# The zero-padded k stationaries of the tails: copied by DVE instead of POOL

## The chip, the cores and the metric

The kernel runs on one core of one Trainium2 chip. The metric is the device time of one execution in microseconds. The engines are TensorE (PE in the profile; its weight loads are PEld), VectorE (DVE), ScalarE (ACT), GpSimd (POOL) and SyncE (SP), which issues the DMAs. Each engine works through its own queue in order, and an instruction that waits for a semaphore holds up those behind it on its engine.

## The reference

An attention with capped scores feeds a gated block. Shapes: q, k, v are 4 x 12 x 448 x 64; x is 4 x 448 x 768; w_in is 768 x 1024, w_sg 448 x 448, w_out 512 x 768, all in float32.

```python
scores = scale * np.matmul(q, k.transpose(0, 1, 3, 2))
scores = cap * np.tanh(scores / cap)
scores = scores - np.max(scores, axis=-1, keepdims=True)
attn = np.exp(scores)
attn = attn / (np.sum(attn, axis=-1, keepdims=True) + 1e-09)
x = np.matmul(attn, v)                    # heads side by side: 448 x 768
h = gelu(x @ w_in)                        # tanh form
u, v = h[..., :512], h[..., 512:]
v_n = (v - mean(v)) / sqrt(var(v) + 1e-06) * g_ln
v_s = np.einsum('ts,bsd->btd', w_sg, v_n) + b_sg[None, :, None]
out = x + (u * v_s) @ w_out
```

## The kernel before

The attention works on pairs of heads: 4 batches of 6 pairs, 24 pairs P in all. A sequence of 448 is three full chunks of 128 keys and a tail of 64 (TL). Each pair has four steps, one for each chunk and one for the tail, in which the tails of both heads share one step of 128 rows. For the pairs after the first the order of a pair's steps is chunk 1, tail, chunk 2, chunk 3 (`unit`, L219). `scores` (L223) writes the scores of one step into one of two PSUM tiles sc; `soft` (L252) and `soft2` (L258) do tanh and exp on ACT into a slot raw; `av` (L266) multiplies with v into pav; `den` (L283) sums the rows on PE, after DVE has added some of the chunks together (`add`, L325, the L328 of the trace).

The scores are made more exact than one pass would be: q and k are split into a rounded part and a rest. Four steps of preparation for the next pair run inside each pair: `prep_a` (q rounded, qs), `prep_k` (k rounded, kh, L172), `prep_b` (rest of q, L180), `prep_c` (rest of k, kl, L188). For the batches 0 and 1 the roundings are on DVE, later on ACT (L157 and L159 in `cast`); the rests are on DVE. For the full chunks PE takes its weights straight from kh and kl (L243). For the tail it takes them from kt (L229): a single buffer of 128 x 2 x 3 x 64, whose middle block is zero, with the tail of head 0 in the first block and that of head 1 in the third. A window of two blocks is then one head's 64 columns beside 64 zero columns, so that the four matmuls of a tail (kh and kl for each head) add up in one tile with the two heads in different rows. The zeros are set once (L694). Two copies fill the blocks for each pair: `kt_hi` (L190) from kh and `kt_lo` (L191) from kl, each 128 x 2 x 64. Each must wait until the tail matmuls of the pair before have read kt.

The gated block of a batch is woven into the attention of the batches after it. `filler` (L551) takes a number of matmuls from a generator between the steps: `norm` (division by den, L365 and L368, and the split of x, L372 to L375), `hv` (L399; gelu and the normalisation, L382 to L426), `hu` (L443; gelu, with L388 writing u), `vsg` (L457, then L466 to L473), `outp` (L486, L491). The weights win, wout and wsg arrive as 64-bit words read by DMA and are decoded while the attention runs (`decode`, L583): one piece is L591 or L594 (DVE early, ACT later), L596, L598, L601 and L604 on DVE, L606 on POOL, L611 on DVE, the rounding L157 or L159, and L613 on POOL. So POOL's queue holds the decoding (L606, L613, and L577 for wsg), the inverse roots of the normalisation (L413) and, before the change, the copies into kt.

The order of instructions on each engine is not that of the code: a scheduler of the framework orders the queues when the program is built, from its own estimate of when each operation can run. Moving two instructions to another engine can therefore move others.

Of the kernel before, what the change touches and what calls it, by code (L numbers as in the profile page):

```python
# [53 lines left out]
def kernel(  # L54
# [15 lines left out]
    nc = tc.nc  # L70
    B, NP, _, _, S = q2.shape
    NC = w_sgT.shape[1]
    FC = S // 128
# [37 lines left out]
    kt_hi, kt_lo = [kt[:, i, ::2, :] for i in range(2)]  # L111

    def f32(ap):
        return ap.bitcast(FP32)
# [18 lines left out]
    def two(t):  # L133
        return t.rearrange("p (a s) -> p a s", a=2)

    raws, qks, vs = {}, {}, {}
# [45 lines left out]
    def prep_c(P):  # L182
        if P >= NPAIR:
            return
        kr = two(raws[P][1])
        kl = qk_p.tile([128, 2, S], FP32R, tag="kl", name="kl")
        eng = nc.gpsimd if P // NP in POOL_KL else nc.vector
        eng.tensor_tensor(out=kl, in0=kr, in1=f32(qks[P][1]), op=ALU.subtract)  # L188
        qks[P].append(kl)
        nc.gpsimd.tensor_copy(out=kt_hi, in_=f32(qks[P][1])[:, :, 128 * FC:])  # L190
        nc.gpsimd.tensor_copy(out=kt_lo, in_=f32(kl)[:, :, 128 * FC:])  # L191
        for t in raws.pop(P):
            raw_s.put(t)

# [506 lines left out]
    for g in range(NSTEP + LAG + 2):  # L701
        P, c = divmod(g, NC)
# [13 lines left out]
        if g < NSTEP:  # L716
            soft2(g)
            if c == 0:
                prep_a(P + 1)
                prep_k(P + 1)  # L720
            elif c == 1:
                prep_b(P + 1)
            elif c == 2:
                prep_c(P + 1)
                load_pair(P + 2)
# [95 lines left out]
```

## Time and profile before

| what | value |
|---|---|
| time, median of 3 runs | 468.64 us (468.02 to 470.51) |
| the profiled execution: its time, its span | 467.07 us, 465.1 us |
| busy: PE, PEld | 442.3 us (95%), 291.8 us (63%) |
| busy: DVE, ACT, POOL | 353.0 us (76%), 291.6 us (63%), 99.1 us (21%) |
| granted TensorE clock, mean | 0.992 |

The rows further down are of four kinds. A row of the windows gives the busy time of each engine in one stretch, with the number of instructions, the granted clock of TensorE, the share of DMA and its rate. A row of the groups gives line, engine and operation, what is written from what, the shapes and the count, then the busy time, the mean of one in ns, and the idle time of the engine just before with what ended it. A row of the timeline gives the start in us from the span's start, the length, the engine, line and operation, the count where equal ones follow each other, and in brackets how long the engine had been idle before it and who ended that. On DVE and ACT one instruction's row can begin before the row above ends, so the distance between two starts can be shorter than a length.

### The profile page before, as it was taken

To read this page: it belongs to the slowest core of one execution; us is meant where nothing else is said; L and a number is where in the kernel's file an instruction comes from. 1 tells how busy PE (TensorE), PEld (TensorE's weight loads), DVE (VectorE), ACT (ScalarE), POOL (GpSimd) and SP (SyncE) were. 2 spreads that over 40 slices of the span, in tenths; PEclk is the share of its full clock that TensorE was granted. 3 is DMA by queue.
4 is the path that set the end of the run, shared out by engine and by line. 5 is a ranking of instruction groups with operands and counts; after the bars stand their busy time and mean duration, and the time that the engine had idled before them with its cause. 6 is when DMAs were issued, how large, how long until landed. Compare 5 with 4: busy or idle time off the path is not lost.

```text
span 465.1 us, 5865 instructions
## 1 busy us (share of the span) xinstructions
PE 442.3 (95%) x2024; PEld 291.8 (63%) x2024; DVE 353.0 (76%) x640; ACT 291.6 (63%) x432; POOL 99.1 (21%) x144
## 2 busy tenths in 40 slices
PE   3999989969999989999999999999999999999996
PEld 0435433345475666665677677766676767778986
DVE  4847998999899888698888557788777455678662
ACT  2659868855786759787678676567778661144410
POOL 1415654265443420410030001000010000000000
PEclk9999998999999999999999999999999999999999
DMA  8457745306212442731230321330320001200002
GB/s 236 172 184 227 246 137 170 109 23 183 93 47 103 136 141 86 238 113 62 81 103 0 117 88 55 135 135 0 108 97 8 17 0 39 75 6 1 0 29 91
DMA packets 20749, 45.23 MB, mean 97 GB/s; under 512 B 3056, under 2 KB 6768, under 8 KB 20720
## 3 DMA queue, kind: packets, MB, share of 16 engines
q1 hardware_dynamic: 20720, 44.86, 29.6%
q8 instruction: 16, 0.26, 0.2%
q14 instruction: 13, 0.11, 0.1%
HBM read 39.35 MB, written 5.51 MB: 96 GB/s over the span
## 4 chain that ended last, share of the span: by engine, by line
PE 57%; DVE 5%; POOL 2%; ACT 1%; issue 1%; POOLq 0%; ACTq 0%
PE gp L486 11%; PE gp L443 10%; PE pav L272 9%; PE gp L399 8%; PE gp L457 8%; PE sc L243 6%; PE sc L229 2%; PE den L291 2%; DVE raw L328 1%; POOL wout L613 1%; POOL raw L606 1%; DVE raw L611 1%; PE gp L365 1%; DVE t L351 1%; DVE xu L368 0%
## 5 line engine op out<-in xcount | busy, mean ns | idle before, releaser
L256 ACT ACTIVATE raw<-sc,qsc 128x896 f32<-128x896 f32 (+1 forms) x96 | 86.1, 909 | 49.2 <-PE sc L243 32.6
L272 PE MATMUL pav<-raw,v 128*64 128x448 f32 x384 | 93.4, 561 | 0.0
L259 ACT ACTIVATE raw<-raw,cap_sb 128x896 f32<-128x896 f32 (+1 forms) x96 | 89.7, 944 | 0.9
L399 PE MATMUL gp<-win,r 128*128 128x512 f32 x264 | 66.5, 400 | 3.3 <-DVE r L373 3.0
L443 PE MATMUL gp<-r,win 128*128 128x448 f32 x288 | 64.1, 371 | 1.4 <-DVE u L388 1.0
L486 PE MATMUL gp<-r,wout 128*128 128x448 f32 x288 | 63.7, 371 | 0.9 <-POOL wout L613 0.5
L399 PEld LDWEIGHTS gp<-win,r 128*128 128x128 f32 x264 | 48.6, 189 | 22.5 <-issue 4.9
L443 PEld LDWEIGHTS gp<-r,win 128*128 128x128 f32 x288 | 53.1, 188 | 14.7 <-issue 7.8
L486 PEld LDWEIGHTS gp<-r,wout 128*128 128x128 f32 x288 | 53.0, 188 | 12.1 <-issue 4.3
L243 PE MATMUL sc<-qs,kh 128*128 128x448 f32 x144 | 55.6, 387 | 1.9 <-DVE kh L200 1.8
L272 PEld LDWEIGHTS pav<-raw,v 128*64 128x64 f32 x384 | 24.6, 138 | 50.4 <-issue 37.9
L243 PE MATMUL sc<-qs,kl 128*128 128x448 f32 x144 | 53.6, 374 | 0.0
L328 DVE TENSOR_TENSOR raw<-raw,raw 128x896 f32<-128x896 f32 (+1 forms) x54 | 47.9, 888 | 4.8 <-PE pav L272 3.3
L457 PE MATMUL gp<-wsg,r 128*128 128x448 f32 x176 | 39.8, 371 | 2.6 <-DVE u L388 2.6
L243 PEld LDWEIGHTS sc<-qs,kh 128*128 128x128 f32 x144 | 27.4, 191 | 19.4 <-ACT raw L256 6.9
L457 PEld LDWEIGHTS gp<-wsg,r 128*128 128x128 f32 x176 | 32.4, 188 | 11.1 <-issue 4.2
L291 PE MATMUL den<-raw,ones_sb 128*32 128x448 f32 x216 | 36.9, 573 | 0.3 <-DVE raw L328 0.3
L190 POOL CAST kt<-kh 128x128 fp32r<-128x128 f32 x23 | 11.7, 508 | 117.1 <-PE sc L229 112.2
L413 POOL TENSOR_TENSOR rs<-rs,pw 128x1 f32<-128x1 f32 (+1 forms) x16 | 9.9, 617 | 102.5 <-DVE rs L412 102.5
L243 PEld LDWEIGHTS sc<-qs,kl 128*128 128x128 f32 x144 | 27.6, 191 | 5.8 <-DVE qs L157 2.1
L188 DVE TENSOR_TENSOR kl<-raw,kh 128x896 fp32r<-128x896 f32 x23 | 27.0, 1174 | 3.2 <-PE den L291 1.8
L613 POOL TENSOR_TENSOR win<-xu,win 128x256 fp32r<-128x256 f32 x22 | 22.8, 1039 | 29.3 <-ACT win L159 16.8
(90 smaller groups left out, 564.4 us busy)
## 6 DMA issues: line engine op xcount, KB each, us to landing
raw<-in_q_dram SPq DMA_DIRECT2D x23, 448.0 KB, 3.5
raw<-in_k_dram SPq DMA_DIRECT2D x23, 448.0 KB, 4.5
v<-in_vp_dram SPq DMA_DIRECT2D x24, 256.0 KB, 3.4
xu<-in_w_in_dram SPq DMA_DIRECT2D x22, 256.0 KB, 4.3
out_dram<-xu SPq DMA_DIRECT2D x24, 224.0 KB, 1.9
raw<-in_w_out_dram SPq DMA_DIRECT2D x11, 256.0 KB, 3.5
u<-in_w_sgT_dram SPq DMA_DIRECT2D x4, 224.0 KB, 5.9
raw<-in_w_in_dram SPq DMA_DIRECT2D x2, 256.0 KB, 4.1
```

Source lines behind the costliest of these rows:

```text
L188: eng.tensor_tensor(out=kl, in0=kr, in1=f32(qks[P][1]), op=ALU.subtract)
L243: nc.tensor.matmul(out=sc[:, h, :S], lhsT=w[:, h, 128 * c - 128:128 * c], rhs=qs[:, h, :], start=(i == 0), stop=(i == 1))
L256: nc.scalar.activation(out=prob(g), in_=src, func=ACTF.Tanh, scale=qsc)
L259: nc.scalar.activation(out=prob(g), in_=prob(g), func=ACTF.Exp, scale=cap_sb)
L272: nc.tensor.matmul(out=pav_t[P][64 * h:64 * h + 64, :S], lhsT=w, rhs=two(p_t[g])[:, h if c else 0, :], start=(g % NC == 0), stop=(c == NC ...
L291: nc.tensor.matmul(out=t[32 * j:32 * j + 32, :S], lhsT=ones_sb[:, 0 if c else 1 + h, NP - 1 - P % NP:NP + 31 - P % NP], rhs=two(src)[:, h ...
L328: eng.tensor_tensor(out=a, in0=a, in1=w, op=ALU.add)
L399: yield 1, lambda i=i, c=c, a=a, w=w: nc.tensor.matmul(out=ps, lhsT=a[c][:, t * 128:t * 128 + 128], rhs=win[w][:, c, HF:], start=(i == 0), ...
L443: yield 1, lambda a=a, w=w, c=c, st=st, sp=sp: nc.tensor.matmul(out=ps, lhsT=win[w][:, c, f * 128:(f + 1) * 128], rhs=a[c][:, :S], start=s ...
L457: yield 1, lambda i=i, c=c, a=a, w=w: nc.tensor.matmul(out=ps, lhsT=a[c][:, f * 128:(f + 1) * 128], rhs=wsg[w][:, c, :], start=(i == 0), s ...
L486: yield 1, lambda ps=ps, c=c, a=a, w=w, f=f, st=st, sp=sp: nc.tensor.matmul(out=ps, lhsT=wout[w][:, f, c * 128:(c + 1) * 128], rhs=a[f][:, ...
L613: nc.gpsimd.tensor_tensor(out=dst[1], in0=f, in1=f32(dst[0]), op=ALU.subtract)
```

## The change

In `prep_c` the two copies into kt are issued on DVE (`nc.vector`) instead of POOL (`nc.gpsimd`). Their shapes, sources and destinations stay.

```diff
@@ -187,8 +187,8 @@
         eng = nc.gpsimd if P // NP in POOL_KL else nc.vector
         eng.tensor_tensor(out=kl, in0=kr, in1=f32(qks[P][1]), op=ALU.subtract)
         qks[P].append(kl)
-        nc.gpsimd.tensor_copy(out=kt_hi, in_=f32(qks[P][1])[:, :, 128 * FC:])
-        nc.gpsimd.tensor_copy(out=kt_lo, in_=f32(kl)[:, :, 128 * FC:])
+        nc.vector.tensor_copy(out=kt_hi, in_=f32(qks[P][1])[:, :, 128 * FC:])
+        nc.vector.tensor_copy(out=kt_lo, in_=f32(kl)[:, :, 128 * FC:])
         for t in raws.pop(P):
             raw_s.put(t)
```

The scheduler's order moves on PE, DVE, ACT, POOL and SP. Three places follow; two smaller ones are told in words. On PE the four matmuls of a tail stand together at some places where they were spread, or a little later, and around 229 us of the trace before DVE's L383 and L426 of the normalisation change places. On DVE the two copies of a pair follow kl, mostly with one to four other instructions in between; for the late pairs they stand after instructions that ran when the tail before had ended.

The first place is DVE at about 155 to 165 us of the trace before, where the first batch's u are made (u_99 is the fourth, t_101 its temporary; raw_67, raw_72 and raw_73 are slots with pieces of wout). Before:

```order
L383 SCALAR_TENSOR_TENSOR t_101<-t_101,gp 128x448
L611 TENSOR_TENSOR raw_72<-raw_72 128x256
L596 TENSOR_SCALAR raw_73<-raw_73 128x256
L598 TENSOR_SCALAR raw_73<-raw_73 128x256
L601 SCALAR_TENSOR_TENSOR raw_73<-raw_73 128x256
L328 TENSOR_TENSOR raw_69<-raw_69,raw_74 128x896
L388 SCALAR_TENSOR_TENSOR u_99<-t_101,gp 128x448
L604 TENSOR_SCALAR raw_73<-raw_73 128x256
```

The same place after the change, with the copies of pair 11 at its head:

```order
L190 CAST kt<-kh 128x2x64
L191 CAST kt<-kl 128x2x64
L611 TENSOR_TENSOR raw_73<-raw_73 128x256
L611 TENSOR_TENSOR raw_67<-raw_67 128x256
L596 TENSOR_SCALAR raw_72<-raw_72 128x256
L598 TENSOR_SCALAR raw_72<-raw_72 128x256
L383 SCALAR_TENSOR_TENSOR t_101<-t_101,gp 128x448
L601 SCALAR_TENSOR_TENSOR raw_72<-raw_72 128x256
L604 TENSOR_SCALAR raw_72<-raw_72 128x256
L611 TENSOR_TENSOR raw_72<-raw_72 128x256
L388 SCALAR_TENSOR_TENSOR u_99<-t_101,gp 128x448
L596 TENSOR_SCALAR raw_73<-raw_73 128x256
```

L388 of u_99 has moved up to stand directly behind the L611 of raw_72; the L596, L598 and L601 of raw_73 and the add L328 now come behind it.

The second place is ACT at about 63 to 74 us of the trace before, at the first weight piece that ACT rounds (win_115 is the rounded w_in, raw_74, raw_69 and raw_72 are the probabilities of three steps). Before:

```order
L256 ACTIVATE raw_74<-sc,qsc 128x896
L594 ACTIVATE xu<-xu 128x256
L259 ACTIVATE raw_74<-raw_74,cap_sb 128x896
L159 ACTIVATE win_115<-xu 128x256
L256 ACTIVATE raw_69<-sc,qsc 128x896
L159 ACTIVATE win_115<-xu 128x256
```

After:

```order
L256 ACTIVATE raw_74<-sc,qsc 128x896
L159 ACTIVATE win_115<-xu 128x256
L259 ACTIVATE raw_74<-raw_74,cap_sb 128x896
L256 ACTIVATE raw_69<-sc,qsc 128x896
L594 ACTIVATE xu<-xu 128x256
L259 ACTIVATE raw_69<-raw_69,cap_sb 128x896
```

The rounding L159 has moved ahead of the exp L259 of raw_74, and the second L159 back behind the exp of raw_69.

The third place is PE at about 101 to 105 us of the trace before, in the first `hv` of the first batch (raw_72 here is a sum of probabilities that DVE's L328 has just written):

```order
 L399 MATMUL gp<-win_116,r_77 128x512
 L399 MATMUL gp<-win_115,r_78 128x512
+L291 MATMUL den<-raw_72,ones_sb 32x448 x2
 L399 MATMUL gp<-win_115,r_79 128x512
 L399 MATMUL gp<-win_116,r_79 128x512
-L291 MATMUL den<-raw_72,ones_sb 32x448 x2
```

The den matmuls of raw_72 have moved up by two L399.

## Rows read from the trace of the kernel before

**Rows 1.** Windows, three stretches: busy PE, PEld, DVE, ACT, POOL, then clock, DMA.

```profile
42.00:67.50 25.50, 25.50 (x142) 11.66 (x140) 22.90 (x50) 22.37 (x33) 15.77 (x19) 1.00 0.64 215
...
106.00:148.00 42.00, 40.97 (x184) 26.50 (x184) 38.69 (x84) 30.22 (x51) 19.04 (x25) 1.00 0.35 115
...
217.00:409.00 192.00, 191.35 (x891) 136.23 (x888) 136.90 (x212) 121.49 (x168) 11.82 (x25) 1.00 0.20 66
```

**Rows 2.** Groups by line and shape: the copies on POOL, and DVE's smallest cast.

```profile
L190 POOL CAST kt<-kh 128x128 fp32r<-128x128 f32 x23 | 11.7, 508 | 117.1 <-PE sc L229 112.2 <-DVE kh L157 3.7 <-issue 1.2
L191 POOL CAST kt<-kl 128x128 fp32r<-128x128 f32 x23 | 10.2, 442 | 21.5 <-DVE kl L188 21.2 <-POOL kt L190 0.3
...
L157 DVE CAST win<-xu 128x256 fp32r<-128x256 f32 x10 | 2.8, 285 | 0.1
```

**Rows 3.** Timeline of DVE, two neighbours in the first norm.

```profile
91.67 0.21 DVE L375 TENSOR_TENSOR r<-xu,r 128x64 fp32r<-128x64 f32 x1
91.81 0.61 DVE L368 TENSOR_TENSOR xu<-xu,gp 128x448 f32<-128x448 f32 x1
```

**Rows 4.** Timeline of DVE and POOL around the copies of pair 20.

```profile
294.90 1.09 DVE L188 TENSOR_TENSOR kl<-raw,kh 128x896 fp32r<-128x896 f32 x1 [1.84 <-PE den L291]
...
307.24 0.61 DVE L368 TENSOR_TENSOR xu<-xu,gp 128x448 f32<-128x448 f32 x1
...
307.65 0.29 POOL L190 CAST kt<-kh 128x128 fp32r<-128x128 f32 x1 [19.69 <-PE sc L229]
```

**Rows 5.** Timeline around PE's first stall: DVE, ACT, PE.

```profile
64.65 0.30 DVE L596 TENSOR_SCALAR xu<-xu 128x256 f32<-128x256 f32 x1 [0.79 <-POOL xu L606]
...
64.99 1.03 ACT L259 ACTIVATE raw<-raw,cap_sb 128x896 f32<-128x896 f32 x1
69.24 0.42 ACT L159 ACTIVATE win<-xu 128x256 fp32r<-128x256 f32 x1 [3.23 <-DVE xu L611]
...
70.70 1.05 PE L229 MATMUL sc<-qs,kt 128*128 128x448 f32 x4 [3.01 <-ACT raw L256]
```

**Rows 6.** Windows, the stretch of that stall; the eighth figure is the granted clock.

```profile
67.00:76.00 9.00, 5.99 (x25) 2.11 (x24) 8.52 (x14) 5.39 (x9) 5.42 (x8) 0.81 0.33 102
```

**Rows 7.** Timeline of PE in the first hv.

```profile
101.67 2.35 PE L399 MATMUL gp<-win,r 128*128 128x512 f32 x6 [2.62 <-DVE r L373]
104.30 1.66 PE L291 MATMUL den<-raw,ones_sb 128*32 128x448 f32 x4 [0.28 <-DVE raw L328]
```

**Rows 8.** Timeline from 146 to 165 us: DVE, ACT, PE.

```profile
146.72 0.42 DVE L611 TENSOR_TENSOR xu<-xu 128x256 f32<-128x256 f32 x1 [0.51 <-POOL xu L606]
...
159.98 0.95 DVE L611 TENSOR_TENSOR raw<-raw 128x256 f32<-128x256 f32 x1 [0.27 <-POOL raw L606]
...
163.96 0.61 DVE L388 SCALAR_TENSOR_TENSOR u<-t,gp 128x448 f32<-128x448 f32 x1
...
160.07 0.57 ACT L387 ACTIVATE t<-t 128x448 f32<-128x448 f32 x1
...
159.95 2.09 PE L457 MATMUL gp<-wsg,r 128*128 128x448 f32 x9
164.63 0.68 PE L457 MATMUL gp<-wsg,r 128*128 128x448 f32 x2 [2.59 <-DVE u L388]
```

**Rows 9.** Timeline of DVE and PE in the second batch's hv.

```profile
228.12 0.68 DVE L383 SCALAR_TENSOR_TENSOR t<-t,gp 128x512 f32<-128x512 f32 x1
229.29 0.69 DVE L426 TENSOR_TENSOR r<-t,r 128x512 fp32r<-128x512 f32 x1 [0.49 <-ACT r L425]
...
234.56 0.55 DVE L423 TENSOR_SCALAR t<-t,mv,rs 128x512 f32<-128x512 f32 x1 [0.44 <-POOL rs L413]
...
238.96 0.47 PE L443 MATMUL gp<-r,win 128*128 128x448 f32 x1 [0.34 <-DVE t L388]
```

**Rows 10.** Timeline of DVE and POOL where two of their operations meet.

```profile
72.66 0.82 DVE L596 TENSOR_SCALAR xu<-xu 128x256 f32<-128x256 f32 x1
...
72.26 1.06 POOL L613 TENSOR_TENSOR win<-xu,win 128x256 fp32r<-128x256 f32 x1 [1.34 <-ACT win L159]
```

## The prediction

> **What bounds the kernel now.** I read the busy time by windows first, then the waits of TensorE (PE), then the lines around its longest waits on each engine. The share of a whole span hides the stages, so the windows decide [rows 1]. From 217 to 409 us PE is busy 191.35 of 192 us and VectorE (DVE) 136.90: what DVE does there counts only where PE waits for that very operation. From 42 to 67.5 us DVE is busy 22.90 of 25.5 us and from 106 to 148 us 38.69 of 42: here a DVE operation more can come out as time, and PE does wait, 3.01 us before 70.70 us and 2.59 us before 164.63 us [rows 5, 8]. So the change is decided before 165 us, by what it does to DVE's queue, and what PE gains or loses there is handed on to the end by the PE-bound stretch behind it.
>
> **The copies themselves.** There are 23 pairs of them, one L190 and one L191 for each head pair after the first. On GpSimd (POOL) they are busy 11.7 and 10.2 us, and POOL waited 112.2 us before L190 for the tail's matmuls L229 and 21.2 us before L191 for kl [rows 2]: that queue has time. All 46 move to DVE. No row shows a 128x128 cast on DVE. The nearest: a 128x256 cast takes 285 ns [rows 2]; and since DVE's instructions overlap at their ends, what counts is the distance to the next start: the 128x64 subtraction at 91.67 us lets the next one start at 91.81 us, 0.14 us [rows 3]. I take 0.14 us a copy, because both neighbours in size agree on it: the 64-column row gives it directly, and half of the 285 ns of a cast with twice the columns is 0.14 us too. The bounds are 0.29 us (the whole 128x256 duration) and 0, a copy in a gap of DVE. Over 46 copies 0.14 us is 6.4 us of DVE, but only those before 165 us can hurt: pairs 1 to 11, 22 copies, 3.1 us.
>
> **The wait that moves with them.** A copy overwrites kt, which the tail's matmuls of the pair before still read. On POOL that wait held up little. On DVE everything queued behind the copy (gating work, adds, weight decoding) would stand, and PE waits for that work. kl of pair 20 was ready at 295.99 us; POOL's copy of that pair stood 19.69 us and started at 307.65 us, when the tail had ended [rows 4]. Right behind kl, a copy would hold DVE for 11.7 us. The changed order does not do that: there the two copies of pair 20 stand behind the L368 that ran from 307.24 to 307.85 us [rows 4], so the tail has ended 0.2 us before. Cost 0; if DVE runs a little ahead, some tenths, and DVE's gaps in the PE-bound part take them.
>
> **First stall of PE, 67 to 71 us.** ACT's cast L159 waits 3.23 us, until 69.24 us, for a weight piece that DVE finishes late (L611); the tanh behind it frees the scores tile for which PE waits until 70.70 us [rows 5]. In the new order the same DVE operations stand ahead of this L611, and from 46 us on six copies more, 6 x 0.14 = 0.84 us. Against that, DVE's L596 at 64.65 us had waited 0.79 us for POOL's L606 [rows 5], which stood in POOL's queue right behind the two copies of pair 6; that goes. The two cancel. ACT's queue changes too: the exp L259 at 64.99 us (1.03 us [rows 5]) now stands behind the waiting cast, ahead of the tanh, so the stall may grow by 1.0 us; or it may shrink by as much if DVE gains from POOL's emptier queue. I take 0, with 1.0 us either way.
>
> **98 to 106 us.** No copy lies between 86 and 106 us. On PE, the den matmuls of raw_72 move ahead of two matmuls L399. Den had waited 0.28 us for DVE's add and started at 104.30 us; the two now come after that wait instead of before it. Six of them took 2.35 us, so two take 0.8 us [rows 7]. PE has other small gaps behind it: I take +0.4, bounds 0 and +0.8.
>
> **106 to 165 us.** Eight copies (pairs 8 to 11) add 8 x 0.14 = 1.1 us to DVE. Some fall into gaps in which DVE waits for POOL's L606, as the 0.51 us at 146.72 us [rows 8]: pairs 10 and 11 have copies just ahead of such a wait, 0.5 us in all. Net +0.6, bounds 0 and 2.3 (8 x 0.29). Then comes the largest term. PE ends a group of L457 at 162.04 us and waits 2.59 us for DVE's L388 of u_99, which runs from 163.96 to 164.57 us [rows 8]. Its input, ACT's L387, was there at 160.64 us; an L611 of DVE ended at 160.93 us [rows 8], and then DVE did an L596, an L598, an L601 and an add L328 ahead of it: 163.96 - 160.93 = 3.03 us. In the new order L388 stands directly behind that L611 and the four come after. It then ends at 164.57 - 3.03 + 0.6 = 162.1 us. PE is free at 162.04 + 0.4 = 162.4 us, so the stall is gone and PE goes on at 162.4 instead of 164.6 us: -2.2 us for everything up to here, the +0.4 and +0.6 included.
>
> **After 165 us.** DVE has gaps that take the copies. At one place the order costs: around 229 us L383 and L426 change places. L426 had waited 0.49 us for ACT behind an L383 of 0.68 us; now that L383 comes after the wait. A later wait of 0.44 us (L423 at 234.56 us) is filled by an add instead, and two copies come on top: 0.68 - 0.44 + 0.28 = +0.5 us. PE had waited 0.34 us for this chain at 238.96 us [rows 9], so it counts.
>
> **Sum.** 0 - 2.2 + 0.5 = -1.7 us. The profiled run took 467.07 us (its span 465.1), 1.6 us under the median of 468.64; the change is set against the median: 468.64 - 1.7 = 466.9 us, 0.4% less. About 0.5% (2.3 us) is what a measurement of this kernel can tell from no change.
>
> **Rivals.**
> *The first stall goes as well (faster by more).* For it: POOL's queue is free of copies that waited, so L606 and with it DVE's L611 come earlier; and TensorE was granted 0.81 of its clock on average from 67 to 76 us [rows 6], so the loss there is the 3.01 us and up to (1 - 0.81) x 9 = 1.7 us. Against: ACT's exp is now behind the waiting cast. Half of 4.7 us on top of 1.7 gives 468.64 - 1.7 - 2.4 = 464.5 us; all of it 462.2 us.
>
> *DVE and POOL hold each other up (slower).* DVE's L596 at 72.66 us took 0.82 us instead of 0.30 (the same operation at 64.65 us) while POOL's L613 ran from 72.26 us for 1.06 us [rows 5, 10]. A copy on DVE that meets an L606 or L613 may cost those 0.52 us more. The Trainium skill, SBUF — State Buffer, section "Who interferes with whom", states this as a rule: of a DVE and a GpSimd operation that need the shared ports, the one that starts first has them for its whole instruction and the other fully blocks; the two rows agree with it. It speaks against the change, since POOL keeps its long operations and DVE gets more that can be blocked. If half of the 22 early copies meet one, 11 x 0.52 = 5.7 us. L388 of u_99 is 0.3 us ahead of PE in my working (162.1 against 162.4 us); from 0.3 us of lateness on, each microsecond of DVE counts. With ACT's 1.0 us in the first stall: 468.64 - 1.7 + (5.7 - 0.3) + 1.0 = 473.3 us. A third of the 5.7, 1.9 us, is likelier, as the DVE operation after the copy would have met the same POOL operation: 468.64 - 1.7 + (1.9 - 0.3) + 1.0 + 0.4 (den at its bound) = 469.9 us. It decides for slower than before once copies and blocking together cost over 2 us more than I count.
>
> *Nothing moves.* POOL had the time, PE is the bound later, and L388's input comes late or another wait takes the place of the 2.59 us: 468.6 us.
>
> **How the numbers follow.** The forecast 0.32 and "nothing moves" 0.11 lie within 0.5%. The first rival 0.37; its mild end (466.3 us) is just under the forecast. The second 0.20. So faster 0.37, same 0.43, slower 0.20. The range leaves out 0.1 on each side: the strongest quarter of the first rival, below 462.8, and the worse half of the second, above 471.2, about midway between its two times.
>
> **What would show it.** Right: no wait of PE for L388 near 162 us; copies on DVE whose next instruction starts 0.14 us later; DVE's waits for L229 under 0.5 us in all. Wrong in size: a PE wait near 67 us of over 4 us, or copies of over 0.5 us on DVE. Wrong in kind: the L388 of u_99 ended late by ACT's L387 and not by DVE, or a new wait of PE before 165 us, which a shift of any of these queues can make.

## The result, and the profile after

The changed kernel takes 470.75 us (median of 20 executions, 468.94 to 473.17), the kernel before 467.34 us (median of 20, 465.39 to 470.88). The ratio is 1.0067 with a 95% interval of 1.0050 to 1.0085: slower by 0.67%, some 3.1 us, where 0.4% less (1.7 us) was forecast. The profiled execution of the changed kernel took 472.34 us, 1.6 us over its median; its span is 470.6 us.

The line of the page that sums up the engines, after:

```profile
PE 448.2 (95%) x2024; PEld 293.6 (62%) x2024; DVE 357.6 (76%) x686; ACT 293.2 (62%) x432; POOL 80.4 (17%) x98
```

DVE has 46 instructions more and is busy 4.6 us longer, as the change says. But PE, with the same number of matmul records (2024), is busy 5.9 us longer than before (448.2 against 442.3). This figure points at the cause, though not all of it is lost time, as will be seen.

The windows of [rows 1], after:

```profile
42.00:67.50 25.50, 25.50 (x141) 11.75 (x139) 24.23 (x55) 20.51 (x30) 12.58 (x12) 1.00 0.64 213
106.00:148.00 42.00, 42.00 (x181) 27.79 (x178) 38.73 (x87) 29.09 (x49) 15.31 (x19) 0.93 0.35 111
217.00:409.00 192.00, 191.99 (x885) 135.34 (x885) 136.52 (x228) 122.59 (x168) 5.08 (x8) 1.00 0.19 63
```

From 217 to 409 us PE is the bound as before, and DVE no busier (136.52 against 136.90 us).

The copies, by line, and four neighbours on DVE's timeline (they answer [rows 2, 3]):

```profile
L191 DVE CAST kt<-kl 128x128 fp32r<-128x128 f32 x23 | 6.1, 265 | 0.0
L190 DVE CAST kt<-kh 128x128 fp32r<-128x128 f32 x23 | 5.5, 240 | 0.2 <-PE sc L229 0.2
...
56.83 0.28 DVE L604 TENSOR_SCALAR xu<-xu 128x256 int32<-128x256 int32 x1
57.03 0.21 DVE L190 CAST kt<-kh 128x128 fp32r<-128x128 f32 x1
57.16 0.22 DVE L191 CAST kt<-kl 128x128 fp32r<-128x128 f32 x1
57.30 0.71 DVE L596 TENSOR_SCALAR xu<-xu 128x256 f32<-128x256 f32 x1
```

Next starts 0.13 and 0.14 us after a copy, and DVE waited 0.2 us in all for the tail's L229: the two small terms were right.

The timeline after at the places of [rows 5, 8], and PE's waits behind each of them:

```profile
68.23 0.42 ACT L159 ACTIVATE win<-xu 128x256 fp32r<-128x256 f32 x1 [2.62 <-DVE xu L611]
70.53 1.08 PE L229 MATMUL sc<-qs,kt 128*128 128x448 f32 x4 [1.06 <-ACT raw L256]
...
79.91 0.47 PE L243 MATMUL sc<-qs,kh 128*128 128x448 f32 x1 [0.32 <-ACT raw L256]
81.41 0.97 PE L272 MATMUL pav<-raw,v 128*64 128x448 f32 x4 [0.42 <-ACT raw L259]
82.95 0.91 PE L291 MATMUL den<-raw,ones_sb 128*32 128x448 f32 x2 [0.57 <-DVE t L349]
...
163.78 0.43 DVE L611 TENSOR_TENSOR raw<-raw 128x256 f32<-128x256 f32 x1 [0.73 <-POOL raw L606]
164.12 0.61 DVE L388 SCALAR_TENSOR_TENSOR u<-t,gp 128x448 f32<-128x448 f32 x1
164.79 0.67 PE L457 MATMUL gp<-wsg,r 128*128 128x448 f32 x2 [0.77 <-DVE u L388]
...
176.23 1.01 ACT L256 ACTIVATE raw<-sc,qsc 128x896 f32<-128x896 f32 x1 [0.74 <-POOL wout L613]
177.28 0.47 PE L243 MATMUL sc<-qs,kh 128*128 128x448 f32 x1 [1.40 <-ACT raw L256]
186.57 0.68 PE L486 MATMUL gp<-r,wout 128*128 128x448 f32 x2 [0.40 <-DVE r L473]
```

Both long waits shrank: at 71 us from 3.01 to 1.06 us, for L388 of u_99 from 2.59 to 0.77 us. New ones stand behind them: 0.32, 0.42 and 0.57 us at 80 to 83 us, 1.40 and 0.40 us at 177 and 187 us. They are not the whole loss, though. From 213 to 246 us PE waits for nothing, and still falls back; its rows there, after, and ahead of them a whole group at 159 us:

```profile
159.39 0.96 PE L291 MATMUL den<-raw,ones_sb 128*32 128x448 f32 x8
...
213.35 1.72 PE L272 MATMUL pav<-raw,v 128*64 128x448 f32 x6
215.00 0.47 PE L365 MATMUL gp<-rds,sel_r 128*128 128x448 f32 x1
215.40 0.97 PE L272 MATMUL pav<-raw,v 128*64 128x448 f32 x2
...
217.72 0.97 PE L272 MATMUL pav<-raw,v 128*64 128x448 f32 x2
218.61 0.47 PE L365 MATMUL gp<-rds,sel_r 128*128 128x448 f32 x1
219.02 1.72 PE L272 MATMUL pav<-raw,v 128*64 128x448 f32 x6
220.67 0.95 PE L291 MATMUL den<-raw,ones_sb 128*32 128x448 f32 x4
221.54 6.19 PE L399 MATMUL gp<-win,r 128*128 128x512 f32 x26
...
234.50 0.95 PE L291 MATMUL den<-raw,ones_sb 128*32 128x448 f32 x4
...
243.69 0.97 PE L272 MATMUL pav<-raw,v 128*64 128x448 f32 x2
244.61 0.47 PE L443 MATMUL gp<-r,win 128*128 128x448 f32 x1
245.01 1.72 PE L272 MATMUL pav<-raw,v 128*64 128x448 f32 x6
```

How to read these: an L272 or L291 leaves two records, so x8 is four matmuls and x2 one alone. A group of L272 is the two heads of one step (x4, so x8 is two groups); a group of L291 is four matmuls (x8). L272 multiplies the two heads of a step into different rows of pav, and the trace of the kernel before, which had such places too, shows what that means. PE's timeline there, around 308 and 312 us:

```profile
307.62 1.72 PE L272 MATMUL pav<-raw,v 128*64 128x448 f32 x8
309.28 0.67 PE L365 MATMUL gp<-rds,sel_r 128*128 128x448 f32 x2
...
312.29 1.72 PE L272 MATMUL pav<-raw,v 128*64 128x448 f32 x6
313.94 2.12 PE L399 MATMUL gp<-win,r 128*128 128x512 f32 x8
315.98 0.97 PE L272 MATMUL pav<-raw,v 128*64 128x448 f32 x2
316.88 2.79 PE L399 MATMUL gp<-win,r 128*128 128x512 f32 x11
```

Four L272 hold PE for 1.66 us until the next starts (307.62 to 309.28), three for 1.65 us (312.29 to 313.94), and the one that was put elsewhere for 0.90 us more (315.98 to 316.88). The two heads run side by side; one alone takes as long as both. For L291, whose four matmuls write four row blocks of den, the rows say the same: in the trace of after, x4 takes 0.95 us (220.67 us) and x8 0.96 us (159.39 us). Each group that other matmuls divide therefore holds PE some 0.9 us longer. In the order of before 16 groups are divided, 5 of them after 200 us; in the changed order 22, 8 of them after 200 us. That makes 6 x 0.9 = 5.4 us, close to PE's 5.9 us, but the closeness is in part luck: PE is also busy longer where its granted clock is low, as in this profiled execution from 104 to 116 us (last section). Pages of runs at the same clock are compared further down. The Trainium skill, TensorE: Matmul & The Clock Gate, section "Part 3: Packing small matmuls — row/col tiling", says that matmuls with few output rows run at the same time when their outputs lie on different groups of partitions, and that matmuls start and end in program order; the rows agree with the first, and no row here tests the second by itself.

To see where time goes without the ups and downs of a place, one more figure is worked out from the records: **PE's lag**. Each matmul counts with the mean time of its line where PE is full (after 240 us in the trace of before); the lag is how much later a kernel's PE has done as much work as PE had done at time t in the trace of before. Where a divided group stands just at the time of a column, as at 212 us, its figure can be off by up to 0.9 us. In us, for the profiled executions of the runs that follow:

```
t (us)                66    75    83   115   160   166   178   188   212   246   325   456
changed kernel      +0.9  -1.7  +0.8  +2.0  +2.0  +0.1  +1.8  +2.7  +2.9  +5.4  +5.5  +5.5
e1_dve_old_order    +1.0  -0.3  +0.6  +0.4  +1.0  +2.4  +2.7  +2.7  +2.8  +2.9  +2.8  +2.9
e2_pool_new_order   +1.3  -1.6  +0.9  -1.0  -0.6  -2.3  -0.6  +0.2  +0.4  +2.9  +2.9  +2.9
e3_u99_alone        +0.8  +1.3  +1.3  +2.6  +2.5  -0.3  +1.6  +1.8  +1.9  +1.9  +1.9  +1.9
e4_new_..._old      +1.9  -1.2  +1.4  +0.4  +0.4  -1.5  +0.3  +0.5  +0.8  +0.8  +0.9  +0.9
e5_old_..._new      +1.3  -0.8  +0.0  -0.5  -0.4  +0.2  +1.7  +2.5  +2.8  +5.3  +5.4  +5.4
e6_new_rejoined     +1.9  -0.8  +1.8  +0.6  +0.5  -1.4  +0.3  +1.1  +0.2  +1.0  +1.0  +1.1
e7_old_rejoined     +1.1  -1.0  -0.2  -1.0  -1.0  -1.0  -1.0  -1.0  -2.2  -1.9  -2.9  -5.2
f3_old_divided      -0.1  +0.1  +0.2  +0.1  +0.0  +0.0  +0.0  +0.3  +0.4  +2.9  +2.9  +3.0
```

### The profile page after: what moved, and what is told of

Read it like the earlier page. It is cut to its first block, busy times and chain, and to the rows that moved or that the text cites. A ratio compares the mean times of both kernels' runs of the same rounds, so it can differ in the third digit from the quotient of the medians.

```text
span 470.6 us, 5809 instructions
## 1 busy us (share of the span) xinstructions
PE 448.2 (95%) x2024; PEld 293.6 (62%) x2024; DVE 357.6 (76%) x686; ACT 293.2 (62%) x432; POOL 80.4 (17%) x98
## 4 chain that ended last, share of the span: by engine, by line
PE 70%; DVE 14%; DMA 4%; ACT 4%; issue 3%; POOL 3%; SPq 0%; POOLq 0%; DVEq 0%; ACTq 0%
PE pav L272 13%; PE gp L399 12%; PE gp L443 11%; PE gp L486 10%; PE sc L243 9%; PE gp L457 6%; PE den L291 5%; PE sc L229 3%; DMA xu<-in_w_in_dram 2%; POOL raw L606 1%; DVE qs L180 1%; ACT raw L256 1%; POOL xu L606 1%; DVE raw L611 1%; DVE kl L188 1%
## 5 line engine op out<-in xcount | busy, mean ns | idle before, releaser
L256 ACT ACTIVATE raw<-sc,qsc 128x896 f32<-128x896 f32 (+1 forms) x96 | 86.1, 908 | 54.1 <-PE sc L243 37.5
L272 PE MATMUL pav<-raw,v 128*64 128x448 f32 x384 | 95.2, 556 | 1.5 <-ACT raw L259 1.5
L259 ACT ACTIVATE raw<-raw,cap_sb 128x896 f32<-128x896 f32 (+1 forms) x96 | 89.7, 944 | 1.0
L399 PE MATMUL gp<-win,r 128*128 128x512 f32 x264 | 67.4, 404 | 2.9 <-DVE r L373 2.6
L399 PEld LDWEIGHTS gp<-win,r 128*128 128x128 f32 x264 | 49.5, 192 | 22.4 <-issue 5.0
L243 PE MATMUL sc<-qs,kh 128*128 128x448 f32 x144 | 55.6, 388 | 4.5 <-DVE kh L200 2.4
L272 PEld LDWEIGHTS pav<-raw,v 128*64 128x64 f32 x384 | 25.1, 136 | 51.4 <-issue 35.3
L243 PE MATMUL sc<-qs,kl 128*128 128x448 f32 x144 | 53.8, 374 | 0.0
L328 DVE TENSOR_TENSOR raw<-raw,raw 128x896 f32<-128x896 f32 (+1 forms) x54 | 48.0, 889 | 5.2 <-PE pav L272 4.2
L243 PEld LDWEIGHTS sc<-qs,kh 128*128 128x128 f32 x144 | 27.4, 191 | 22.4 <-ACT raw L256 8.5
L291 PE MATMUL den<-raw,ones_sb 128*32 128x448 f32 x216 | 39.6, 558 | 1.0 <-DVE t L349 0.6
L243 PEld LDWEIGHTS sc<-qs,kl 128*128 128x128 f32 x144 | 27.5, 191 | 6.5 <-DVE qs L157 2.1
L491 DVE TENSOR_TENSOR xu<-xu,gp 128x448 f32<-128x448 f32 x24 | 14.6, 611 | 18.2 <-PE gp L486 18.0
L613 POOL TENSOR_TENSOR win<-xu,win 128x256 fp32r<-128x256 f32 x22 | 22.7, 1034 | 33.7 <-DVE win L157 19.8
```

The source lines that it names most:

```text
L243: nc.tensor.matmul(out=sc[:, h, :S], lhsT=w[:, h, 128 * c - 128:128 * c], rhs=qs[:, h, :], start=(i == 0), stop=(i == 1))
L256: nc.scalar.activation(out=prob(g), in_=src, func=ACTF.Tanh, scale=qsc)
L259: nc.scalar.activation(out=prob(g), in_=prob(g), func=ACTF.Exp, scale=cap_sb)
L272: nc.tensor.matmul(out=pav_t[P][64 * h:64 * h + 64, :S], lhsT=w, rhs=two(p_t[g])[:, h if c else 0, :], start=(g % NC == 0), stop=(c == NC ...
L291: nc.tensor.matmul(out=t[32 * j:32 * j + 32, :S], lhsT=ones_sb[:, 0 if c else 1 + h, NP - 1 - P % NP:NP + 31 - P % NP], rhs=two(src)[:, h ...
L328: eng.tensor_tensor(out=a, in0=a, in1=w, op=ALU.add)
```

## Experiments: the engine or the order

The move changes two things at once: the engine of the copies, and the scheduler's order on every engine. To part them, the runs below fix the order. At the end of the program a table names, for each engine, its instructions in the wanted order, and an edge that orders without waiting ties each one behind the one before:

```python
for queue in table:
    for a, b in zip(queue, queue[1:]):
        tc.add_manual_dep(by[f"I-{b}"], f"I-{a}", info(), reason="queue")
```

**e1, copies on DVE, old order.** The edit beside the table of before:

```diff
-        nc.gpsimd.tensor_copy(out=kt_hi, in_=f32(qks[P][1])[:, :, 128 * FC:])
-        nc.gpsimd.tensor_copy(out=kt_lo, in_=f32(kl)[:, :, 128 * FC:])
+        nc.vector.tensor_copy(out=kt_hi, in_=f32(qks[P][1])[:, :, 128 * FC:])
+        nc.vector.tensor_copy(out=kt_lo, in_=f32(kl)[:, :, 128 * FC:])
+        pin(tc, OLD_ORDER)
```

> The copies run on DVE, but every other instruction stands in its engine's queue where it stood in the kernel before; each copy stands in DVE's queue ahead of the first instruction that started after POOL's copy had started in the trace of before. Theory of order (what is lost is lost because the move makes the scheduler put other instructions elsewhere): no change from the kernel before, 467.3 us, ratio 0.998 to 1.003. Theory of DVE's time (each copy makes DVE's chain later by its own distance of 0.13 to 0.14 us, and 22 of them lie before 165 us): ratio 1.004 to 1.007, that is up to 3.1 us more. Theory of mutual blocking between DVE and POOL: as the second, and the sum of DVE's instruction times beside POOL's L606 and L613 grows by more than the copies themselves.

Measured: 468.49 us against 467.32 us, ratio 1.0006 (0.9976 to 1.0035). No change: the copies on DVE cost nothing that can be measured, at most the 1.6 us of the interval's upper end, where DVE's time alone was to cost 1.9 to 3.3 us. Nor is the sign of blocking there: all of DVE's busy time rose by 3.9 us (356.9 against 353.0 us), with 46 instructions more that take 0.22 us each.

**e2, copies on POOL, new order.** The edit undone, the table that of the changed kernel:

```diff
-        nc.vector.tensor_copy(out=kt_hi, in_=f32(qks[P][1])[:, :, 128 * FC:])
-        nc.vector.tensor_copy(out=kt_lo, in_=f32(kl)[:, :, 128 * FC:])
+        nc.gpsimd.tensor_copy(out=kt_hi, in_=f32(qks[P][1])[:, :, 128 * FC:])
+        nc.gpsimd.tensor_copy(out=kt_lo, in_=f32(kl)[:, :, 128 * FC:])
+        pin(tc, NEW_ORDER)
```

> The reverse: the copies run on POOL as before, but every other instruction stands in its queue where it stands in the changed kernel; each copy stands in POOL's queue at the place that belongs to its start on DVE in the trace of the changed kernel. Theory of order: as slow as the changed kernel, ratio 1.005 to 1.009 (470 to 471.5 us). Theory of DVE's time or of blocking: the loss goes with the copies, ratio 0.998 to 1.002.

Measured: 470.04 us, ratio 1.0048 (1.0019 to 1.0076). The loss stays with the order, just under the expected 1.005 to 1.009. Theories of DVE's time and of blocking fall: with the copies back on POOL the loss should have gone.

**e4 and e5, the order of one side of 170 us.** Copies on DVE in both; the table takes what starts before 170 us from one order and the rest from the other:

```diff
+        pin(tc, NEW_ORDER_TO_170_THEN_OLD)      # e4
+        pin(tc, OLD_ORDER_TO_170_THEN_NEW)      # e5
```

> The copies on DVE. The changed kernel's order for all that starts before 170 us, the old order (as in the first of these runs) for the rest. At 165 us the lag of PE's work behind the kernel before was only 0.16 us in the profiled executions, and 5.3 us came after that. If it is the order after 170 us that loses: ratio 0.998 to 1.002 (about 467.5 us). If the copies' time on DVE loses, wherever the order is from: ratio 1.004 to 1.008. If the order before 170 us loses in most executions and the two profiles mislead: 1.004 or more as well, with PE waits before 165 us that add up to over 2 us more than in the kernel before.

> The copies on DVE. The old order for all that starts before 170 us, the changed kernel's order for the rest. If the order after 170 us loses: ratio 1.006 to 1.011 (the kernel before plus 3 to 5.3 us). If the order ahead of 170 us loses, or the loss after it only comes from what is late there: ratio 0.998 to 1.003.

Measured: e4 468.04 us, ratio 1.0001 (0.9971 to 1.0030); e5 472.31 us, ratio 1.0092 (1.0060 to 1.0124). What loses is the order after 170 us. That of before 170 us is worth nothing beyond the 1.4 us either way of e4's interval. The lag of e5 grows by 1.1 us from 178 to 212 us and by 2.5 us from there to 246 us, as in the changed kernel (1.1 and 2.5) and in e2 (1.0 and 2.5).

In e2, e4 and e6 (below) the profiled execution had the same mean clock, 0.999. So the busy time of PE can be compared, in this order:

```profile
PE 446.1 (95%) x2024; PEld 292.2 (62%) x2024; DVE 351.2 (75%) x640; ACT 293.6 (63%) x432; POOL 99.0 (21%) x144
PE 443.7 (95%) x2024; PEld 291.9 (63%) x2024; DVE 358.1 (77%) x686; ACT 292.3 (63%) x432; POOL 79.9 (17%) x98
PE 443.2 (95%) x2024; PEld 291.7 (63%) x2024; DVE 357.4 (77%) x686; ACT 293.5 (63%) x432; POOL 80.3 (17%) x98
```

Against e2, with 22 divided groups, e4 has three fewer and 2.4 us less, e6 four fewer and 2.9 us less: 0.7 to 0.8 us a group.

**e3, L388 of u_99 alone.** The prediction's largest term by itself, in the order of before, copies on POOL (DVE's queue):

```diff
 L611 TENSOR_TENSOR raw_72<-raw_72 128x256
+L388 SCALAR_TENSOR_TENSOR u_99<-t_101,gp 128x448
 L596 TENSOR_SCALAR raw_73<-raw_73 128x256
 L598 TENSOR_SCALAR raw_73<-raw_73 128x256
 L601 SCALAR_TENSOR_TENSOR raw_73<-raw_73 128x256
 L328 TENSOR_TENSOR raw_69<-raw_69,raw_74 128x896
-L388 SCALAR_TENSOR_TENSOR u_99<-t_101,gp 128x448
```

> The kernel before, copies on POOL, one instruction moved: DVE's L388 of u_99 stands directly behind the L611 that starts at 159.98 us, ahead of the L596, L598, L601 and L328. By the prediction's largest term: PE's 2.59 us wait at 164.63 us goes and 2.2 us are won, 465.1 us, ratio 0.993 to 0.997. By the rival that the gain is given back (in the run with the new order to 170 us and the old one behind it, PE was 1.45 us ahead at 165 us and 0.33 us behind at 178 us, with new waits for L466 and for ACT's L256): ratio 0.998 to 1.001, with PE waits of over 1 us between 165 and 180 us.

Measured: 465.48 us against 467.22 us, ratio 0.9972 (0.9942 to 1.0003). Between the two: the medians differ by 1.7 us, the interval just reaches no change. PE's timeline shows the wait gone and two others in its place:

```profile
168.64 0.68 PE L457 MATMUL gp<-wsg,r 128*128 128x448 f32 x2 [1.04 <-DVE t L466]
177.03 0.47 PE L243 MATMUL sc<-qs,kh 128*128 128x448 f32 x1 [0.33 <-ACT raw L256]
```

The lag falls by 2.8 us at 166 us and grows by 1.9 us to 178 us. What was put behind L388 (L596 to L328) now runs from 164.08 to 166.58 us, and an L611 behind it waits 0.78 us for POOL's L606, so L466 starts at 167.91 us: most of the gain is handed back 4 to 12 us later.

## Experiments: divided groups

**e6, the changed kernel with four groups put together.** All on PE between 213 and 246 us; one of the four:

```diff
-L272 MATMUL pav<-raw_70,v 64x448
+L272 MATMUL pav<-raw_70,v 64x448 x2
 L443 MATMUL gp<-r_82,win_115 128x448
-L272 MATMUL pav<-raw_70,v 64x448
 L272 MATMUL pav<-raw_71,v 64x448 x2
```

> The changed kernel, copies on DVE, all queues as they are there but for PE between 213 and 246 us: three pairs of L272 (the two heads of one step) that other matmuls divide stand together again, and one group of four L291. Theory of divided groups: two L272 of one step run side by side, and one that stands alone takes as long as a pair (0.90 us from its start to the next); each division costs PE 0.9 us, so 4 x 0.9 = 3.6 us come back: 467.2 us, ratio 0.998 to 1.002. Theory that the loss after 213 us is waiting for the late chain of the second batch (L383, L410 to L426): no change against the changed kernel, ratio 1.005 to 1.009.

Measured: 468.12 us against 467.22 us, ratio 1.0024 (1.0001 to 1.0047); the changed kernel's median is 2.6 us above it (2.0 us by the two ratios), where 3.6 us were expected back. Two to three of the four are won: from 188 to 246 us the lag of the changed kernel grows by 2.7 us, that of e6 falls by 0.1. L399, brought forward, waits 0.19 us for DVE's L368 at 217.77 us in e6, so part of the gain meets the DVE chain. The theory of the late chain of the second batch, which expected no change, falls.

**f3, the reverse.** The kernel before, with three groups divided and nothing else (PE's queue):

```diff
-L272 MATMUL pav<-raw_75,v 64x448 x2
+L272 MATMUL pav<-raw_75,v 64x448
 L243 MATMUL sc<-qs,kh 128x448
 L399 MATMUL gp<-win_115,r_82 128x512
 L399 MATMUL gp<-win_116,r_82 128x512
 L399 MATMUL gp<-win_115,r_84 128x512
+L272 MATMUL pav<-raw_75,v 64x448
...
-L291 MATMUL den<-raw_72,ones_sb 32x448 x2
 L272 MATMUL pav<-raw_69,v 64x448 x2
 L272 MATMUL pav<-raw_68,v 64x448 x2
+L291 MATMUL den<-raw_72,ones_sb 32x448 x2
```

> The reverse test: the kernel before, copies on POOL, nothing changed but PE's order at three places, where it divides three groups as the changed kernel's order does after 213 us: one L272 behind three L399, two L291 behind four L272, one L272 behind three L443. Theory of divided groups: 3 x 0.9 = 2.7 us more, 469.9 us, ratio 1.004 to 1.0075. If divisions cost nothing: 0.998 to 1.002.

Measured: 470.06 us against 467.28 us, ratio 1.0072 (1.0045 to 1.0099), 2.8 us for three. PE's busy time in its page, 2.9 us over that of before, and the divided L291 in its timeline:

```profile
PE 445.2 (95%) x2024; PEld 292.3 (62%) x2024; DVE 353.4 (75%) x640; ACT 291.8 (62%) x432; POOL 98.0 (21%) x144
...
231.03 0.95 PE L291 MATMUL den<-raw,ones_sb 128*32 128x448 f32 x4
231.90 1.72 PE L272 MATMUL pav<-raw,v 128*64 128x448 f32 x8
233.56 0.95 PE L291 MATMUL den<-raw,ones_sb 128*32 128x448 f32 x4
234.43 2.83 PE L399 MATMUL gp<-win,r 128*128 128x512 f32 x11
```

Half a group takes 0.87 us to the next start, twice. With copies and every other queue untouched, three such moves on PE make a loss as large as the whole change did.

**e7, the kernel before with its own five late groups put together** (at 211, 313, 340, 373 and 393 us), edits as in e6, copies on POOL:

```diff
-L272 MATMUL pav<-raw_75,v 64x448
+L272 MATMUL pav<-raw_75,v 64x448 x2
 L399 MATMUL gp<-win_115,r_91 128x512
...
-L272 MATMUL pav<-raw_75,v 64x448
```

> The kernel before, copies on POOL, all queues as they are there but for PE after 200 us: the four pairs of L272 and the one group of L291 that are divided there stand together. Theory of divided groups: 5 x 0.9 = 4.5 us less, 462.8 us, ratio 0.989 to 0.993. If a division costs nothing because PE waits or overlaps there: ratio 0.998 to 1.002.

Measured: 462.03 us against 467.22 us, ratio 0.9901 (0.9862 to 0.9939). PE's busy time and the place of 312 us:

```profile
PE 437.4 (95%) x2024; PEld 291.3 (63%) x2024; DVE 351.8 (76%) x640; ACT 291.6 (63%) x432; POOL 99.4 (22%) x144
...
310.48 1.73 PE L272 MATMUL pav<-raw,v 128*64 128x448 f32 x8
312.13 4.60 PE L399 MATMUL gp<-win,r 128*128 128x512 f32 x19
```

4.9 us of PE less than before, and the lag falls at each of the five places.

**e8, the changed kernel with thirteen groups put together** from 60 us on, eight of them after 200 us; edits as in e6.

> The changed kernel, copies on DVE, with nine pairs of L272 and four groups of L291 put together on PE from 60 us on (two groups of L291 before 110 us stay divided). Theory of divided groups: eight of the thirteen lie after 200 us, 8 x 0.9 = 7.2 us less than the changed kernel, and the five early ones give nothing or up to 0.9 us each where PE does not wait: 462 to 463.6 us, ratio 0.988 to 0.992. If waiting in the late part is what counts: ratio over 1.000.

Measured: 464.16 us, ratio 0.9926 (0.9898 to 0.9954), a little over the expected 463.6 and 6.6 us under the changed kernel. The eight late ones (7.2 us) explain it; the five early ones gave nothing that shows. That PE meets its waits for DVE behind them is the likely reason, and was not tried. Of the L291 groups from 60 us on that stay divided, one stands at 83 us and one at 127 us, not both before 110 us.

**f1 and f2, the best of the old order with the copies on either engine.** The five groups of e7 and the L388 of e3 together; in f2 the copies are on DVE as in e1:

```diff
+        pin(tc, OLD_ORDER_REJOINED_U99)                     # f1, copies on POOL
+        pin(tc, OLD_ORDER_REJOINED_U99_WITH_COPIES)         # f2, copies on DVE
```

> The kernel before, copies on POOL, with two edits of order: the five groups after 200 us put together, and L388 of u_99 moved up. Alone they gave 5.2 and 1.7 us. If they add: 467.2 - 6.9 = 460.3 us, ratio 0.983 to 0.988. If PE, brought forward, meets DVE's and ACT's chains and waits for them again: 462 us, ratio 0.988 to 0.991.

> As the run before it, but with the copies on DVE, each at the place in DVE's queue that belongs to its start on POOL in the trace of before. With the order held still, this is the change by itself, in a kernel that waits less. Theory of order: the same time as with the copies on POOL, within 0.3%. Theory of DVE's time: 22 copies of 0.13 to 0.14 us before 165 us, up to 3.1 us (0.7%) more.

Measured: f1 461.97 us, ratio 0.9868 (0.9834 to 0.9902); f2 462.24 us, ratio 0.9881 (0.9846 to 0.9915). f1's ratio lies in the first range and its median at the second value, 0.1 us from e7, so whether the two edits add is not decided; in its trace PE waits 1.31 us for L466 behind the place of u_99, as in e3. With the order held, DVE and POOL differ by 0.3 us between the medians, well inside either interval (1.6 us each way). This is the change by itself for a second time, and no difference shows; with six executions each, one of a microsecond could not be told.

**f4, f1 and six early groups as well** (L272 at 11, 21, 33 and 88 us, L291 at 110 and 119 us):

```diff
-L291 MATMUL den<-raw_69,ones_sb 32x448
...
-L291 MATMUL den<-raw_69,ones_sb 32x448
+L291 MATMUL den<-raw_69,ones_sb 32x448 x2
```

> As f1, and also four pairs of L272 and two groups of L291 before 170 us put together (at 11, 21, 33 and 88 us, and at 110 and 119 us). PE is busy throughout from 42 to 67 us and from 106 to 126 us, so the ones at 110 and 119 us should give 0.9 us each; but what PE wins there meets the waits for DVE behind it. If all of it is won: 2 to 5 us less than f1; if PE only waits longer for DVE: the time of f1 within 0.3%.

Measured: 461.00 us, ratio 0.9844 (0.9809 to 0.9879). 1.0 us under f1 by the medians, less than the 2 to 5 us of the one case, and inside the interval of f1: it counts as the other case. It is the fastest of all by its median, 1.6% under the kernel before by the ratio and 2% under the changed one by the medians.

## Why the prediction was wrong, point by point

- **What bounds the kernel.** Half right. PE is the bound after 217 us, and DVE's work there hardly counts. But "the change is decided before 165 us" does not follow: PE's own order also moved after that, and where PE is the bound every 0.9 us that it takes longer is time. Nor is what PE gains before 165 us handed on to the end: most of it was given back by 178 us.
- **The copies, 0.14 us each.** Right in size (0.13 and 0.14 us) and without weight: e1 and, against f1, f2 show no cost. The +0.6 us from 106 to 165 us was within what can't be measured.
- **The wait that moves with them.** Right: 0.2 us in all for L229.
- **First stall, 0 with 1.0 us either way.** Too careful at the place: PE's wait fell from 3.01 to 1.06 us and the clock from 67 to 76 us rose from 0.81 [rows 6] to 1.00. L159 ran 1.0 us earlier. But PE's lag, -1.7 us at 75 us, was +0.8 again at 83 us: the three waits at 80 to 83 us make 1.3 us of that, and an L272 that stands alone at 75.97 us, in a group that is whole in the order of before, another 0.9. In sum the 0 was close.
- **98 to 106 us, +0.4.** The L291 of raw_72 there waited 0.44 us at 105.48 us against 0.28 before. The term is small, but this order difference was the hint that was missed: it was read as two matmuls that move past two others, and not as what a matmul alone or in a group costs. Nor do the places listed with the change name the groups of L272 and L291 that the new order divides on PE, early or late.
- **L388 of u_99, -2.2 us for all up to 165 us.** About right at the place: the lag at 166 us is -2.3 in e2 and -1.5 in e4, and +0.1 in the changed kernel's profiled execution, in which PE ran at a lower clock around 110 us (below). Not foreseen: e2, e3 and e4 give back 1.7 to 1.9 us by 178 us, where DVE's and ACT's chains are late; in the changed kernel ACT's L256 at 176.23 us stood behind the decoding of a piece of wout (L613), and PE's wait of 1.40 us came of that. In e5, where PE had waited 2.82 us for u_99, there is no wait at that place; its growth of 1.5 us from 166 to 178 us comes with a clock of 0.79 from 164 to 172 us. So the term was worth little in the end.
- **After 165 us, +0.5. This is the step that failed.** The prediction looked at one exchange on DVE (L383 and L426), took the rest as covered by DVE's gaps, and put PE's own order there at nothing. The exchange itself cost nothing: the 0.34 us for which PE had waited at 238.96 us is there in e1 and e4 (old order) and gone in the changed kernel, e2, e5 and e6, where PE waits for nothing from 225 to 246 us. By e5 the new order after 170 us costs 0.92%, 4.3 us; by e4 all that lies ahead of it is worth 0.0, 1.4 us either way. e2, which has the new order at full clock, shows the step alone: its lag is -2.3 us at 166 us, where -2.2 was forecast, and +2.9 at the end, so 5.2 us are lost after 165 us and not 0.5. (That -2.3 meets -2.2 is in part luck: the clock was 0.81 from 67 to 76 us [rows 6] and 0.88 from 102 to 116 us in the trace of before, 1.00 in both in e2.) Of the 5.2 us, 1.7 are the giving back up to 178 us, 1.0 follow up to 212 us and 2.5 up to 246 us. In the lag of the changed kernel the growth behind the giving back is 1.1 us from 178 to 212 us (PE's 0.40 us for L473 in it) and 2.5 us from 212 to 246 us: the three more divided groups, 3 x 0.9 = 2.7, which cost 2.8 us by themselves in f3.
- **Rivals.** "The first stall goes as well" came true in part, and was handed back; what is left of it is the clock, whose mean has a median of 0.996 over the changed kernel's 20 executions and of 0.991 over 35 of the kernel before (those beside e1). "DVE and POOL hold each other up" had the right sign and the wrong cause: the copies have medians of 219 and 220 ns, and only a few were held long (up to 752 and 770 ns); e1 and f2, which keep the copies on DVE beside the same POOL work, cost nothing; e2, with the copies back on POOL, loses. The third rival, nothing moves, is the truth for the copies themselves.
- **What would show it.** The signs listed were waits, and the length of a copy on DVE. The loss that decided it was busy time of PE. The page's first line gives a hint of it, 442.3 against 448.2 us with equal counts, but not a proof: e3, which divides no group and is not slower, shows 444.3 us, in an execution with a mean clock of 0.988. The surer sign could be read ahead of any run in the order of PE's queue, where x2 had become two rows.

What stays open: of the 3.6 us of e6's four groups 0.8 us (by the lag), 1.0 (by the medians) or 1.6 (by the ratios) did not come back, of which the rows show 0.19 us as a wait; and which exchange of the new order makes the 1.1 us from 178 to 212 us was not tried by itself.

## What to carry to other kernels

When a scheduler orders the queues, an edit of a few instructions is an edit of every queue: compare the order on the engine that is the bound first, and cost what moved there before what was moved on purpose. On PE look for matmuls that run side by side because they write different rows, and count how many of their groups are divided: here each cost some 0.9 us where PE was the bound, and five of those that had been in the kernel all along were worth 1%; early ones, with waits of PE behind them, gave nothing that shows. A wait that goes on PE is only won if the engines behind it are ready; look 10 us further on before you count it.

## What the runs showed of the hardware that was not expected

One L272 alone took PE as long as the two heads' together: 0.97 us for x2 at 215.40 us, 0.97 us for x4 at 81.41 us. Two L291 took 0.95 us and four 0.96 us.

The granted clock differed between executions at the same place. Behind a wait for L388 at about 165 us PE went on at full clock in the kernel before, and at the lower of its two levels, 1.2 GHz, in e1. The windows from 164 to 172 us (columns as in [rows 1]), first of before, then of e1, and the first rows of e1's PE behind the wait:

```profile
164.00:172.00 8.00, 7.37 (x35) 5.52 (x36) 7.16 (x14) 4.31 (x7) 2.30 (x5) 1.00 0.25 73
```

```profile
164.00:172.00 8.00, 6.18 (x23) 5.37 (x25) 5.83 (x12) 3.16 (x6) 1.34 (x2) 0.79 0.30 116
...
165.82 1.11 PE L457 MATMUL gp<-wsg,r 128*128 128x448 f32 x2 [2.80 <-DVE u L388]
166.73 0.57 PE L243 MATMUL sc<-qs,kh 128*128 128x448 f32 x1
167.10 0.57 PE L243 MATMUL sc<-qs,kl 128*128 128x448 f32 x1
```

L243 follows L243 after 0.37 us here (0.20 us in the kernel before, at 165.15 us), and the lag of e1 grows from +1.0 to +2.4 us at this place. e5 shows the same fall, 0.79 from 164 to 172 us after a wait of 2.82 us; f3 and e7, after 2.60 and 2.58 us, went on at 1.00. In the changed kernel's profiled execution the clock fell at another place, 0.72 from 104 to 116 us, after a wait of 2.58 us for DVE's L373 at 103.80 us, where e2 and e4 had 1.00 from 102 to 116 us. So the lag of one profiled execution holds 1 to 2 us that another one has not, and a verdict needs the medians.
